# Sliding-window attention into an eight-expert MoE: late scatters ahead of later rooms' gathers, weight halves on one engine, scales built apart from row numbers

## The chip, the cores and the metric

One core of one Trainium2 chip runs the whole program in one launch. The metric is the device time of that launch in microseconds (us), lower is better. Engines are named as in the profile: PE multiplies matrices, ACT and DVE work on rows of 128 partitions, POOL does small elementwise work and issues every indexed DMA (gather, scatter), SP issues the plain DMAs.

## The reference

Attention of 8 batches, 8 heads, 576 tokens, 64 wide, with a window of 128 and a linear bias, and behind it a mixture of 8 experts:

```
scores = q @ k.T / 8 + bias          # only 0 <= i - j < 128
attn   = softmax(scores) @ v         # 8 x 8 x 576 x 64
x      = attn laid out as 8 x 576 x 512
logits = x @ w_gate ; local = sigmoid(x @ w_local)
for each batch, for s in 0..575:
    e = argmax(logits[s]) if s == 0 or local[s] < 0.5 else the expert of s - 1
    out[s] = softmax(logits[s])[e] * (relu(x[s] @ w1[e]) @ w2[e])
```

w1 is 8 x 512 x 1024, w2 is 8 x 1024 x 512, everything in fp32.

## The kernel before

**Attention, room by room.** A batch is called a room, numbered 0 to 7; a room has four slots of two heads. Each slot's atoms stand in a hand-written string (`ORDER`): scores `S`, row maximum on DVE, exponent on ACT, transposes and the product with v on PE. Generators that do other work are advanced at marks between the atoms: `.` is the routing of the room before (its `route`, its row copies and its entries), and from room 5 on `;` is `early`, `,` is `turns` and `:` is `gathers`. `queued` pins the order in which an engine's instructions were written, so an engine meets its instructions in that order, and an instruction that waits holds all that stand behind it on its engine.

**Routing.** For a room, `route` finds each token's expert, counts the tokens of each expert before it (`OH`, the one-hot of the choice, times a triangle on PE, plus the running counter row `ohs`), and writes each token's row number and its factor into `pay`. Five `enter` scatters of POOL (L725, `t<-pay,to`) put them into a table in HBM (`t4`, `t_76` in the order), sorted by expert. Entries not made at once wait in the list `late`. On POOL the room's outputs are also scaled (`product`, `T<-T,rn`, 128 x 576, four in a room) before SP stores them to `xd`, from which rows are gathered again.

**Experts.** The expert phase is a row of visits. Visits 0 to 3 take 384, 256, 256 and 256 tokens of four experts ("own", 36 columns of table) out of what rooms 0 to 4 hold. `early` does their tables once room 4 is entered: it raises the counters `ohs` of the four experts to the next full block (L877 to L884: for each, two tensor_scalar and one 1x1 add), loads four pieces of the table (`load_table`, L217, `xs<-t`, which waits for every entry made so far), spreads them over the partitions on PE and ACT (`copies`: `pk<-xs,rep`, `xt`), and `indices` makes of them row numbers to gather from (`xidx`) and, through `fw` on POOL and a reduce `sg` on DVE, scales and row numbers to scatter to. `gathers` then fetches visit 0's 12 pieces of rows into a spare buffer (`wraw<-xd,xidx`), and `turns` transposes its three tiles (`xtr`, L203, on DVE) and halves them into a rounded high part and a rest (`qx`, L207 on ACT and L209 on DVE).

**What a visit does.** `h<-qx,cut` and `y<-cut,hh` are its two products (L1100 to L1102, three matmuls for each block: high by high, high by low, low by high). ACT makes the high half of `h` (`hh`, L1205). A weight chunk is loaded by SP into one of six raw buffers (`wraw<-w`, L285), and `split_chunk` cuts it: ACT casts (L295), a subtract makes the rest (L297), on DVE for all halves but number `POOL_CUT = 19`, which POOL does.

**Order in the expert phase.** `Feed.tick` is called between blocks of matmuls. It advances room 7's routing (`side`), and every third tick or so sends one indexed DMA: a gather of a later visit's rows, or `other`, which is a scatter of finished rows (`out<-y`, L1085) or one of the `late` entries. It takes these by turns:

```
ahead_of = self.at < len(self.items) and self.items[self.at][0] <= upto or self.odd
first, second = (self.gather, self.other) if ahead_of else (self.other, self.gather)
```

**The tables of the last visits.** `rank_tables` runs at the end of `side`. It waits until `late` is empty and loads eight further pieces of the table (L217, the first two of 80 and 76 columns) for the experts ordered by their counts. These loads stand on SP in one queue with the weight loads, and wait for every entry.

Of the kernel before, what the change touches and what calls it, by code (L numbers as in the profile page):

```python
# [8 lines left out]
F32 = mybir.dt.float32  # L9
# [4 lines left out]
ALU = mybir.AluOpType  # L14
AX = mybir.AxisListType
PS = bass.MemoryType.PSUM
P = 128

NB = 8
S = 576  # L20
DM = 512
NE = 8
# [3 lines left out]
OWN = [(7, 384), (2, 256), (1, 256), (6, 256)]  # L26
# [5 lines left out]
BPE = 160  # L32
# [36 lines left out]
]  # L69
PLACE = [0, 8, 2, 1, 4, 3, 6, 5, 7]  # L70
DEPTH = 3
POOL_CUT = 19
HALVED = 8
FAR = 2.0 ** 40
Z_HOLD = -1.5 * 2.0 ** -23


@with_exitstack
def moe_attention(ctx, tc, qT, kT_d, vv, vt, wg, wl, w1, w2, out):
# [6 lines left out]
    tp = ctx.enter_context(tc.tile_pool(name="tok", bufs=2))  # L86
# [14 lines left out]
    own = cp.tile([P, NE], F32, name="own")  # L101
    caps = cp.tile([P, NE], F32, name="caps")
    rest = cp.tile([P, NE], F32, name="rest")
    starts = cp.tile([P, NE], F32, name="starts")
    msel = cp.tile([P, 4], F32, name="msel")
    roff = cp.tile([P, 1], F32, name="roff")
# [15 lines left out]
    ohs = st.tile([P, NE], F16, name="ohs")  # L122
# [65 lines left out]
    now = Now()  # L188
# [27 lines left out]
    def load_table(c0, n, block):  # L216
        ins = nc.sync.dma_start(xs[:, c0:c0 + n], t4v[:, block:block + n] if isinstance(block, int) else t4v[:, bass.ds(block, n)])  # L217
        for other in entered:
            tc.add_manual_dep(ins.ins, other.ins.name, mybir.DependencyInfo(mybir.DependencyClass.Sync, mybir.DependencyReason.DATA), reason="entries")
# [5 lines left out]
            tensor.matmul(pk[:, :m].rearrange("p c w -> p (c w)"), rep, xs[:, c:c + m].rearrange("p c w -> p (c w)"), start=True, stop=True)  # L225
            scalar.copy(xt[:, c:c + m], pk[:, :m])

    def indices(vector, c0, n, w0, wins, aid=None):

        aid = aid or vector  # L230
        vector.tensor_tensor(xidx[:, c0:c0 + n], xt[:, c0:c0 + n, 0], roff.broadcast_to([P, n]), ALU.add)
        yield
        m = len(wins)
        f = tp.tile([P, 48, 2, 4], F32, name="fw", bufs=1)[:, :m]
        lo = 0
        while lo < m:
            hi = lo + 1
            while hi < m and wins[hi] == wins[hi - 1] + 4:
                hi += 1
            for w in range(2):  # L240
                aid.tensor_tensor(f[:, lo:hi, w], xt[:, wins[lo]:wins[lo] + 4 * (hi - lo), 1 + w].rearrange("p (c q) -> p c q", q=4),
                                     msel.unsqueeze(1).broadcast_to([P, hi - lo, 4]), ALU.mult)
            lo = hi
            yield
        vector.tensor_reduce(sg[:, w0:w0 + m], f, AX.X, ALU.add)
        vector.tensor_copy(sidx[:, w0:w0 + m], sg[:, w0:w0 + m, 0])
        yield
# [42 lines left out]
                              reason="behind the values")  # L290
        return t

    def split_chunk(raw, c, scalar, vector, n):
        for f in range(2):
            scalar.copy(c[:, 0, f], raw[:, f])  # L295
            yield
            (pool if 2 * n + f == POOL_CUT else vector).tensor_tensor(c[:, 1, f], raw[:, f], c[:, 0, f], ALU.subtract)  # L297
            yield

    class Stream:  # L300
# [22 lines left out]
        def split(self, c, scalar, vector):  # L323
            raw = self.raw.pop(0)
            self.cut[self.n_cut] = c[:, 0], c[:, 1]
            self.n_cut += 1
            yield from split_chunk(raw, c, scalar, vector, self.n_cut - 1 if self is W else 0)

        def find(self, which):
            return min(i for i in self.cut if self.order[i][1] == which)  # L330
# [35 lines left out]
    with ExitStack() as actx:  # L366
# [271 lines left out]
        def lay_rows(b, g, copy):  # L638
            rows, rb = RN[b % 2][:, 0:72].rearrange("p (k i z) -> p k i z", k=4, z=2), RB[b % 2]
            for o in range(2):  # L640
                for z in range(2):
                    c = 64 * (g ^ o) + 32 * z
                    for a in range(2):
                        q = 64 * g + 32 * a
                        copy[a % len(copy)](rows[q:q + 32, :, o::2, z], rb[c:c + 32, :, o:9:2])

        def last_sums():
            b = NB - 1
            invert(b)
            yield  # L650
            both_engines = [dve.tensor_copy, act.copy]
            lay_by_head(b, both_engines)
            yield
            for g in range(2):
                lay_rows(b, g, both_engines)
                yield

        def tokens(b, xT):

# [38 lines left out]
        def scaled(b):  # L698

            if b < NB - 1:  # L700
                while b not in inverted:
                    yield
                for g in range(2):
                    lay_rows(b, g, [pool.tensor_copy])
                    yield
            stores.append(b)
            laid.append(b)
            if b == NB - 1:
                for _ in range(4 * now.calm):
                    yield  # L710
                for p in range(4):
                    product(b, p)
                    yield
                store(b)
# [22 lines left out]
        def in_turns(entries, products):  # L737
            entries, products = list(entries), list(products)
            while entries or products:
                if entries:  # L740
                    e = entries.pop(0)
                    if e == "row":
                        next(prep[":"], None)
                    else:
                        enter(*e)
                if products:
                    e = products.pop(0)
                    if e == "rest":
                        for _ in range(4):
                            pool.memset(spacer, 0.0)  # L750
                    else:
                        product(*e)

        def behind_choices(b):
            if b == NB - 2:
                in_turns(["row"] * 2 + late[:2], [(b, p) for p in range(4)])
                del late[:2]
            if b > NB - 3:
                return
            if b == NB - 3:  # L760
                in_turns(late + ["row"] * 4, [(b, p) for p in range(4)])
            else:
                in_turns(late, [(b, 0)] if b + 1 in EARLY else [(b, 0), (b, 1)])
            late.clear()

        def behind_counts(b):
            n = NT if b + 1 in EARLY else 3 if b < NB - 3 else 0
            late.extend((b, t) for t in range(n, NT))
            if n:
                in_turns([(b, t) for t in range(n)], [(b, p) for p in range(1 if n == NT else 2, 4)])  # L770
            elif b < NB - 1:
                k = 2 if b == NB - 3 else 4
                in_turns(["row"] * k, ["rest"] * (k - 1))

        def both(main, other):

# [93 lines left out]
        def early(group):  # L870
            while EARLY[group[0]] - 1 not in routed:
                yield
            while now.held:
                yield
            pn = ptk.tile([P, NE], F32, name="pk")
            pe.matmul(pn, onesb, ohs, start=True, stop=True)
            for i in group:  # L877
                e, k = OWN[i]
                d = tp.tile([P, 1], F32, name="ed")
                dve.tensor_scalar(d, pn[:, e:e + 1], -1.0, float(k + 32 * BPE * e), ALU.mult, ALU.add)  # L880
                dve.tensor_scalar(d, d, 0.0, None, ALU.max)
                dve.tensor_tensor(ohs[0:1, e:e + 1], ohs[0:1, e:e + 1], d[0:1], ALU.add)
                bumped.append(i)
                load_table(col_of[i], OWN_BLOCKS[i], BPE * e)  # L884
            while slot < LATE + 2 or now.held:
                yield
            copies(pe, act, col_of[group[0]], sum(OWN_BLOCKS[i] for i in group))
            yield
            for i in group:
                yield from indices(dve, col_of[i], OWN_BLOCKS[i], win_of[i], wins_of[i], pool)  # L890
                known.append(i)

        def gathers():

# [35 lines left out]
        side, prep = iter(()), {":": setup(), ";": iter(())}  # L930
        pairs = {}
        LATE = 4 * EARLY[0] + 4
        sums, SUMS = last_sums(), ("C1", "C2", "M1", "M2")

        def spread(order):
            for i, atom in enumerate(order.split()):
# [63 lines left out]
    def rank_tables():  # L1000
# [27 lines left out]
            nc.vector.tensor_scalar(efx[:, f:f + NE], er, 0.0, None, ALU.add)  # L1028
        yield
        while late:  # L1030
            yield
        for a, z, wait in ((0, 2, 8), (2, NE, 14)):
            for r in range(a, z):
# [284 lines left out]
    class Feed:  # L1318
# [52 lines left out]
        def tick(self, upto, turn=True):  # L1371

            self.clock += 1
            next(self.side, None)
            if route_done:
                now.act = nc.scalar
            if next(self.step, 0) == 0 and turn:
                self.turn(upto, 8 if upto == 1 else 10 if upto <= len(EARLY) else self.LAG)
            if upto > len(EARLY):
                self.drain()  # L1380
                self.gather(upto)
                if pending and self.clock % 3 == 0:
                    send()
            elif self.clock >= self.free:
                ahead_of = self.at < len(self.items) and self.items[self.at][0] <= upto or self.odd
                first, second = (self.gather, self.other) if ahead_of else (self.other, self.gather)
                if first(upto) or second(upto):
                    self.free, self.odd = self.clock + 2, not self.odd
# [92 lines left out]
```

## Time and profile before

| quantity | value |
|---|---|
| time, median of 3 runs | 693.24 us (693.11 to 694.29) |
| profiled execution: its time, its span | 693.75 us, 692.1 us |
| mean granted PE clock | 0.965 of full speed |
| PE busy | 650.5 us, 94% |
| DVE, ACT, POOL busy | 456.2, 417.3, 350.2 us |
| q1 (plain DMAs), q0 (indexed DMAs), share of 16 engines | 49.3%, 9.7% |

The time is the median of three runs; durations are read in the profiled execution, whose span is 692.1 us and whose own time is 1.65 us longer. Attention lasts until about 225 us, the end of attention and the first visit overlap until about 255 us, the rest is experts. PE is busy 94% of the span, so what can be saved without less matmul work is its idle time (41.6 us) and the time in which its clock was granted below full speed.

### The profile page before, as it was taken

To read this page: it belongs to the slowest core of one execution; us is meant where nothing else is said; L and a number is where in the kernel's file an instruction comes from. 1 tells how busy PE (TensorE), PEld (TensorE's weight loads), DVE (VectorE), ACT (ScalarE), POOL (GpSimd) and SP (SyncE) were. 2 spreads that over 40 slices of the span, in tenths; PEclk is the share of its full clock that TensorE was granted. 3 is DMA by queue.
4 is the path that set the end of the run, shared out by engine and by line. 5 is a ranking of instruction groups with operands and counts; after the bars stand their busy time and mean duration, and the time that the engine had idled before them with its cause. 6 is when DMAs were issued, how large, how long until landed. Compare 5 with 4: busy or idle time off the path is not lost. (4 is left out here: it accounts for less than half of the span.)

```text
span 692.1 us, 17132 instructions
## 1 busy us (share of the span) xinstructions
PE 650.5 (94%) x5928; PEld 536.7 (78%) x5928; DVE 456.2 (66%) x1445; ACT 417.3 (60%) x1239; POOL 350.2 (51%) x572
## 2 busy tenths in 40 slices
PE   8999999997959789996799999999999999999995
PEld 4777777775747668885689988888888888888884
DVE  6686876878637868883678856573645657476561
ACT  6889899896848674462556635363545455445541
POOL 6354655556363672676177776555463626141011
PEclk9999999998969879999799999999999999999998
DMA  7554784783766257542887856676675748455710
GB/s 232 187 187 149 237 270 150 230 265 108 250 197 201 83 162 256 160 147 82 310 260 245 254 184 180 200 248 201 205 240 170 261 155 289 143 171 166 273 35 32
DMA packets 50363, 134.42 MB, mean 194 GB/s; under 512 B 11015, under 2 KB 13703, under 8 KB 47970
## 3 DMA queue, kind: packets, MB, share of 16 engines
q1 hardware_dynamic: 40754, 113.43, 49.3%
q0 software_dynamic: 9088, 19.29, 9.7%
q8 instruction: 47, 0.77, 0.5%
q10 hardware_dynamic: 432, 0.59, 0.3%
q14 instruction: 42, 0.34, 0.2%
HBM read 113.67 MB, written 19.65 MB: 193 GB/s over the span
## 5 line engine op out<-in xcount | busy, mean ns | idle before, releaser
L197 POOL DMA_INDIRECT kr<-xd,xidx x137 | 155.3, 1133 | 58.5 <-issue 40.6
L297 DVE TENSOR_TENSOR cut<-wraw,cut 128x512 fp32r<-128x512 f32 x215 | 139.3, 685 | 51.2 <-ACT cut L295 50.2
L295 ACT CAST cut<-wraw 128x512 fp32r<-128x512 f32 x198 | 113.2, 617 | 46.7 <-PE y L1102 33.2
L1100 PE MATMUL h<-qx,cut 128*128 128x256 f32 (+8 forms) x440 | 139.5, 317 | 0.0
L1102 PE MATMUL h<-qx,cut 128*128 128x256 f32 (+8 forms) x440 | 138.2, 314 | 0.0
L1101 PE MATMUL h<-qx,cut 128*128 128x256 f32 (+8 forms) x440 | 138.2, 314 | 0.0
L172 ACT ACTIVATE cut<-scs,mn 128x192 f32<-128x192 f32 (+2 forms) x288 | 123.7, 434 | 22.4 <-DVE mn L172 21.6
L1100 PE MATMUL y<-cut,hh 128*128 128x512 f32 (+2 forms) x288 | 114.0, 396 | 9.8 <-ACT hh L1205 9.8
L1085 POOL DMA_INDIRECT out<-y,sidx x41 | 43.9, 1070 | 145.4 <-ACT y L1112 116.2
L1101 PE MATMUL y<-cut,hh 128*128 128x512 f32 (+2 forms) x288 | 113.8, 395 | 0.0
L1102 PE MATMUL y<-cut,hl 128*128 128x512 f32 (+2 forms) x288 | 113.2, 393 | 0.0
L1205 ACT ACTIVATE hh<-h 128x256 fp32r<-128x256 f32 (+7 forms) x104 | 46.0, 443 | 107.4 <-PE h L1102 107.0
L172 DVE CUSTOM_DVE_ANT_0 scs<-sc,bias 128x192 f32<-128x192 f32 (+2 forms) x288 | 84.2, 323 | 34.3 <-PE sc L172 19.7
L1206 DVE SCALAR_TENSOR_TENSOR hl<-h,hh 128x256 fp32r<-128x256 f32 (+8 forms) x112 | 55.6, 497 | 76.7 <-ACT hh L1205 71.9
L1100 PEld LDWEIGHTS h<-qx,cut 128*128 128x128 f32 x440 | 83.4, 190 | 12.9 <-issue 8.4
L172 PE MATMUL sc<-kr,qx 64*64 64x192 f32 (+2 forms) x1280 | 75.3, 315 | 12.2 <-DVE mn L172 11.7
L1101 PEld LDWEIGHTS h<-qx,cut 128*128 128x128 f32 x440 | 83.5, 190 | 3.7
L1102 PEld LDWEIGHTS h<-qx,cut 128*128 128x128 f32 x440 | 83.4, 190 | 0.1
L1100 PEld LDWEIGHTS y<-cut,hh 128*128 128x128 f32 (+2 forms) x288 | 53.8, 187 | 18.9 <-ACT hh L1205 10.2
L172 PEld LDWEIGHTS sc<-kr,qx 64*64 64x64 f32 x1280 | 45.8, 137 | 28.1 <-DVE mn L172 16.2
L172 PE MATMUL pt<-ident,cut 128*128 128x128 f32 x384 | 64.2, 292 | 1.0 <-ACT cut L172 0.7
L1102 PEld LDWEIGHTS y<-cut,hl 128*128 128x128 f32 (+2 forms) x288 | 53.7, 186 | 13.1 <-DVE hl L1206 0.5
(198 smaller groups left out, 936.1 us busy)
## 6 DMA issues: line engine op xcount, KB each, us to landing
wraw<-w SPq DMA_DIRECT2D x112, 512.0 KB
xT<-w SPq DMA_DIRECT2D x10, 1024.0 KB
kr<-kT SPq DMA_DIRECT2D x31, 288.0 KB
qx<-qT SPq DMA_DIRECT2D x30, 288.0 KB
xd<-T SPq DMA_DIRECT2D x7, 1152.0 KB
v<-v SPq DMA_DIRECT2D x22, 256.0 KB
v<-v SPq DMA_DIRECT2D x32, 128.0 KB
cut<-v SPq DMA_DIRECT2D x10, 256.0 KB
```

Of the source, the lines that this page charges most:

```text
L172: ins = getattr(self.engine, name)(*args, **kw)
L197: queued(nc.gpsimd.indirect_dma_start(out=r, out_offset=None, in_=src[0:n, :], in_offset=bass.IndirectOffsetOnAxis(ap=col, axis=0), bounds ...
L295: scalar.copy(c[:, 0, f], raw[:, f])
L297: (pool if 2 * n + f == POOL_CUT else vector).tensor_tensor(c[:, 1, f], raw[:, f], c[:, 0, f], ALU.subtract)
L1085: ins = nc.gpsimd.indirect_dma_start(out=out[:, :], out_offset=bass.IndirectOffsetOnAxis(ap=col[0:n], axis=0), in_=y[0:n], in_offset=None, ...
L1100: nc.tensor.matmul(o, ah, bh, start=start, stop=False)
L1101: nc.tensor.matmul(o, ah, bl, start=False, stop=False)
L1102: nc.tensor.matmul(o, al, bh, start=False, stop=stop)
L1205: now.act.activation(hh, hp, AF.Relu)
L1206: nc.vector.scalar_tensor_tensor(hl, hp, 0.0, hh, ALU.max, ALU.subtract)
```

## The change

Six edits. (1) The own tables' row numbers `xidx` are made in one instruction for all 36 columns, and the scales (`scales`: `fw` on POOL, `sg` on DVE) wait for a later slot (`LATE + 5`, the second slot of room 6), with twelve steps of the generator between POOL's part and DVE's. (2) The counters are raised by a subtract and a max over all eight experts on DVE and one add on POOL, in place of twelve DVE instructions. (3) No weight half is cut on POOL. (4) Row copies of the last room's sums move out of `last_sums` into the room's own side work. (5) The gathers of visit 0 come in fours: four with room 5's products as before, four behind room 5's counts, four with room 6's products; late entries that stood among them move behind room 6's counts. (6) In the expert phase a late entry goes ahead of gathers for later visits, and `rank_tables` waits ten ticks more once `late` is empty.

```diff
-POOL_CUT = 19
+WAIT = 10
...
-    def indices(vector, c0, n, w0, wins, aid=None):
-        aid = aid or vector
+    def indices(vector, c0, n, w0, wins):
         vector.tensor_tensor(xidx[:, c0:c0 + n], xt[:, c0:c0 + n, 0], roff.broadcast_to([P, n]), ALU.add)
         yield
+        yield from scales(vector, vector, w0, wins)
+    def scales(vector, aid, w0, wins):
         m = len(wins)
...
+        if aid is not vector:
+            for _ in range(12):
+                yield
         vector.tensor_reduce(sg[:, w0:w0 + m], f, AX.X, ALU.add)
...
-            (pool if 2 * n + f == POOL_CUT else vector).tensor_tensor(c[:, 1, f], raw[:, f], c[:, 0, f], ALU.subtract)
+            vector.tensor_tensor(c[:, 1, f], raw[:, f], c[:, 0, f], ALU.subtract)
...
             lay_by_head(b, both_engines)
             yield
-            for g in range(2):
-                lay_rows(b, g, both_engines)
-                yield
...
             if b == NB - 1:
-                for _ in range(4 * now.calm):
+                for g in range(2):
                     yield
+                    yield
+                    lay_rows(b, g, both_engines)
...
             if b == NB - 2:
-                in_turns(["row"] * 2 + late[:2], [(b, p) for p in range(4)])
-                del late[:2]
+                in_turns(["row"] * 4, [(b, p) for p in range(4)])
...
-                k = 2 if b == NB - 3 else 4
-                in_turns(["row"] * k, ["rest"] * (k - 1))
+                what = ["row"] * 4 if b == NB - 3 else late[:4]
+                in_turns(what, ["rest"] * 3)
+                if b == NB - 2:
+                    del late[:4]
...
+            d = tp.tile([P, NE], F32, name="ed", bufs=1)
+            dve.tensor_tensor(d, own, pn, ALU.subtract)
+            dve.tensor_scalar(d, d, 0.0, None, ALU.max)
+            pool.tensor_tensor(ohs[0:1], ohs[0:1], d[0:1], ALU.add)
             for i in group:
-                e, k = OWN[i]
-                d = tp.tile([P, 1], F32, name="ed")
-                dve.tensor_scalar(d, pn[:, e:e + 1], -1.0, float(k + 32 * BPE * e), ALU.mult, ALU.add)
-                dve.tensor_scalar(d, d, 0.0, None, ALU.max)
-                dve.tensor_tensor(ohs[0:1, e:e + 1], ohs[0:1, e:e + 1], d[0:1], ALU.add)
                 bumped.append(i)
-                load_table(col_of[i], OWN_BLOCKS[i], BPE * e)
+                load_table(col_of[i], OWN_BLOCKS[i], BPE * OWN[i][0])
...
-            for i in group:
-                yield from indices(dve, col_of[i], OWN_BLOCKS[i], win_of[i], wins_of[i], pool)
-                known.append(i)
+            c0, n = col_of[group[0]], sum(OWN_BLOCKS[i] for i in group)
+            dve.tensor_tensor(xidx[:, c0:c0 + n], xt[:, c0:c0 + n, 0], roff.broadcast_to([P, n]), ALU.add)
+            known.extend(group)
+            while slot < LATE + 5:
+                yield
+            yield from scales(dve, pool, win_of[group[0]], [w for i in group for w in wins_of[i]])
...
         while late:
             yield
+        for _ in range(WAIT):
+            yield
...
-                ahead_of = self.at < len(self.items) and self.items[self.at][0] <= upto or self.odd
+                ahead_of = self.at < len(self.items) and self.items[self.at][0] <= upto or self.odd and not late
```

Lines move down by 6 at L285 and L297 and by 11 at L1085 and L1100; the entries' L725 becomes L731.

**POOL in room 5.** The engine is POOL, the place is the end of room 5's products and what stands behind them; `wraw<-xd,xidx` are the gathers of visit 0's rows, `T` a product, `fw` the first half of the scales, `pay` to `ohs` room 5's row numbers and counts. Before:

```order
L197 DMA wraw<-xd,xidx 128x128
L172 TENSOR_TENSOR T_162<-T_162,rn_97 128x18x32
L172 TENSOR_TENSOR fw<-xt,msel 128x2x4 x4
L172 TENSOR_TENSOR pay<-gt,rse 128x5
L172 TENSOR_TENSOR ri<-ri,cblk 128x5
L172 TENSOR_TENSOR to<-ri,ki 128x5
```

and of the changed kernel:

```order
L197 DMA wraw<-xd,xidx 128x128
L172 TENSOR_TENSOR T_162<-T_162,rn_97 128x18x32
L172 TENSOR_TENSOR pay<-gt,rse 128x5
L172 TENSOR_TENSOR ri<-ri,cblk 128x5
L172 TENSOR_TENSOR to<-ri,ki 128x5
L172 TENSOR_TENSOR ohs<-ohs,cn 128x8
L197 DMA wraw<-xd,xidx 128x128
L172 MEMSET spacer 128x1 x4
L197 DMA wraw<-xd,xidx 128x128
L172 MEMSET spacer 128x1 x4
L197 DMA wraw<-xd,xidx 128x128
L172 MEMSET spacer 128x1 x4
```

The four small `fw` products no longer stand between the scaled rows and room 5's row numbers; they are part of one `fw` pair that comes behind the next four gathers, and two more gathers have moved up to that place.

**DVE in room 6.** The engine is DVE, the place is the one-hot `OH` of room 6's choices; `xtr` is the transposed tile of visit 0, `hr0` the scan of the sticky choice, `scs,mn` the scores with their row maximum. Before:

```order
854 L172 ISA mn_4883 128x1
855 L172 SCALAR_TENSOR_TENSOR hr0_105<-hold_4930,hr0_105,pk_4918 1x64
856 L203 STREAM_TRANSPOSE xtr_4965<-wraw_159 128x512
857 L209 TENSOR_TENSOR qx_4513<-xtr_4965,qx_4513 128x4x128
858 L172 TENSOR_TENSOR OH_4817<-pk_4968,k8_82 128x40
```

and of the changed kernel:

```order
837 L172 ISA mn_4871 128x1
838 L172 SCALAR_TENSOR_TENSOR hr0_105<-hold_4918,hr0_105,pk_4906 1x64
839 L203 STREAM_TRANSPOSE xtr_4953<-wraw_159 128x512
840 L172 TENSOR_TENSOR OH_4803<-pk_4956,k8_82 128x40
841 L172 ISA scs_4966,mn_4871<-sc_4925,bias_134 128x192
```

The transposition stands ahead of `OH` in both. Before it is visit 0's second tile, now the third and last; its `qx` now stands eleven rows behind `OH`.

**POOL and SP around room 7's entries.** The engine is POOL, the place is visit 1, the last stretch of entries; `kr<-xd,xidx` are gathers of later visits' rows. Before:

```order
L725 DMA t_76<-pay,to 40960x4
L197 DMA kr<-xd,xidx 128x128
L725 DMA t_76<-pay,to 40960x4
L197 DMA kr<-xd,xidx 128x128 x3
L1085 DMA out<-y,sidx 4608x512 x2
L725 DMA t_76<-pay,to 40960x4 x3
L1085 DMA out<-y,sidx 4608x512 x2
```

and of the changed kernel, from room 7's counts:

```order
L172 TENSOR_TENSOR ohs<-ohs,cn 128x8
L197 DMA kr<-xd,xidx 128x128
L731 DMA t_76<-pay,to 40960x4
L197 DMA kr<-xd,xidx 128x128 x7
L1096 DMA out<-y,sidx 4608x512
L731 DMA t_76<-pay,to 40960x4 x4
L1096 DMA out<-y,sidx 4608x512
```

Before, ten of the entries of rooms 5 to 7 stand behind room 7's counts, one by one between gathers; now five do, all of room 7. On SP, the two first tables of the last visits stand before:

```order
L285 DMA wraw<-w 128x1024 x2
L217 ISA
L217 DMA xs<-t_76 32x80
L217 ISA
L217 DMA xs<-t_76 32x76
L351 TENSOR_LOAD efx
```

and in the changed kernel:

```order
L217 ISA
L217 DMA xs<-t_76 32x80
L217 ISA
L217 DMA xs<-t_76 32x76
L1046 TENSOR_LOAD efx
L1046 ISA x2
L217 ISA
L217 DMA xs<-t_76 32x56
L1046 TENSOR_LOAD efx
L1046 ISA x2
L291 DMA wraw<-w 128x1024 x2
```

The same tables stand two weight loads earlier in SP's queue, with a third table behind them: the two loads that stood ahead now stand behind.

## Rows read from the trace of the kernel before

**Rows 1.** What PE waited for: us in total, times, longest.

```profile
PE sc L172 <- DVE mn L172: 11.7, 5, 6.9
...
PE y L1100 <- ACT hh L1205: 9.8, 1, 9.8
...
PE pk L172 <- DVE OH L172: 3.8, 7, 2.0
...
PE xa L172 <- ACT xT L172: 2.8, 2, 1.8
```

**Rows 2.** Stretches: length, busy of PE, PEld, DVE, ACT, POOL, PEclk, DMA.

```profile
170.51:176.44 5.93, 5.93 (x67) 4.41 (x67) 3.71 (x19) 5.30 (x21) 3.61 (x4) 0.57 0.51 201
...
232.94:250.62 17.68, 10.68 (x116) 6.98 (x112) 11.60 (x43) 9.73 (x33) 12.21 (x27) 0.71 0.24 86
...
250.62:254.18 3.56, 3.56 (x11) 3.33 (x11) 3.56 (x7) 3.56 (x7) 2.95 (x3) 0.50 0.81 208
...
332.35:335.94 3.59, 3.59 (x11) 2.85 (x12) 2.90 (x6) 2.07 (x5) 0.00 (x0) 0.50 0.92 325
...
335.94:680.00 344.06, 344.06 (x1872) 298.48 (x1872) 215.92 (x391) 173.86 (x365) 164.48 (x147) 1.00 0.62 204
```

**Rows 3.** Timeline of DVE: one transposition that each room has, rooms 4 to 7.

```profile
122.82 0.57 DVE L172 STREAM_TRANSPOSE T<-xT 128x384 f32<-128x384 f32 x1
...
149.65 0.57 DVE L172 STREAM_TRANSPOSE T<-xT 128x384 f32<-128x384 f32 x1
...
182.48 0.57 DVE L172 STREAM_TRANSPOSE T<-xT 128x384 f32<-128x384 f32 x1
...
220.78 0.57 DVE L172 STREAM_TRANSPOSE kr<-xT 128x384 f32<-128x384 f32 x1
```

**Rows 4.** Timeline of DVE and POOL, counters being raised: start, us, instruction.

```profile
165.86 1.64 DVE L172 TENSOR_TENSOR ohs<-ohs,ed 1x1 f16<-1x1 f16 x1
...
167.79 0.15 DVE L172 TENSOR_TENSOR ohs<-ohs,ed 1x1 f16<-1x1 f16 x1
...
166.28 1.20 POOL L172 TENSOR_TENSOR T<-T,rn 128x576 f32<-128x576 f32 x1
```

**Rows 5.** Timeline of SP and PE: the own tables.

```profile
176.88 1.73 SPq L217 DMA_DIRECT2D xs<-t  x4
...
183.96 0.51 PE L172 MATMUL pk<-xs,rep 32*128 32x144 f32 x2
```

**Rows 6.** Timeline of DVE: the reduce of the scales, with its wait.

```profile
200.07 0.17 DVE L172 TENSOR_REDUCE sg<-fw 128x4 f32<-128x16 f32 x1 [7.66 <-POOL fw L172]
```

**Rows 7.** Timeline of POOL and DVE: visit 0's second tile, room 6's choice.

```profile
229.87 1.04 POOL L197 DMA_INDIRECT wraw<-xd,xidx  x1 [0.16 <-issue]
...
232.46 0.71 DVE L203 STREAM_TRANSPOSE xtr<-wraw 128x512 f32<-128x512 f32 x1 [1.28 <-DMA wraw<-xd,xidx]
...
235.01 0.18 DVE L172 TENSOR_TENSOR OH<-pk,k 128x40 f16<-128x40 f32 x1
...
235.50 1.74 DVE L172 TENSOR_TENSOR rch<-rex,OH 128x40 f32<-128x40 f32 x1
```

**Rows 8.** Timeline of ACT: casts of weight halves, and its longest wait.

```profile
311.25 1.14 ACT L295 CAST cut<-wraw 128x512 fp32r<-128x512 f32 x2
...
330.88 1.14 ACT L295 CAST cut<-wraw 128x512 fp32r<-128x512 f32 x2 [13.50 <-DMA wraw<-w]
```

**Rows 9.** Timeline of SP: tables and the weight loads around them.

```profile
323.46 0.89 SPq L217 DMA_DIRECT2D xs<-t  x2
...
326.93 0.83 SPq L285 DMA_DIRECT2D wraw<-w  x2
```

**Rows 10.** Timeline of POOL: first and last entry behind room 7's counts.

```profile
285.36 1.03 POOL L725 DMA_INDIRECT t<-pay,to  x1 [0.49 <-issue]
...
321.24 0.91 POOL L725 DMA_INDIRECT t<-pay,to  x1 [0.30 <-issue]
```

**Rows 11.** Gathers by shape, POOL 285 to 325 us: busy, mean ns, idle before.

```profile
L197 POOL DMA_INDIRECT kr<-xd,xidx x13 | 14.8, 1138 | 4.0 <-issue 3.7 <-DMA kr<-xd,xidx 0.3
```

More of the change, by code (lines that the diff above doesn't have):

```diff
@@ L291, in load_chunk, with split_chunk @@
         return t
-    def split_chunk(raw, c, scalar, vector, n):
+    def split_chunk(raw, c, scalar, vector):
         for f in range(2):
@@ L326, in split @@
             self.n_cut += 1
-            yield from split_chunk(raw, c, scalar, vector, self.n_cut - 1 if self is W else 0)
+            yield from split_chunk(raw, c, scalar, vector)
         def find(self, which):
@@ L645, in lay_rows @@
                         copy[a % len(copy)](rows[q:q + 32, :, o::2, z], rb[c:c + 32, :, o:9:2])
+        both_engines = [dve.tensor_copy, act.copy]
         def last_sums():
@@ L650, in last_sums @@
             yield
-            both_engines = [dve.tensor_copy, act.copy]
             lay_by_head(b, both_engines)
             yield
-            for g in range(2):
-                lay_rows(b, g, both_engines)
-                yield
         def tokens(b, xT):
@@ L932, in moe_attention @@
         LATE = 4 * EARLY[0] + 4
-        sums, SUMS = last_sums(), ("C1", "C2", "M1", "M2")
+        sums, SUMS = last_sums(), ("C1", "C2")
         def spread(order):
```

## The prediction, made before the changed kernel ran

> **What bounds the kernel now.** I first looked for a stretch in which PE never waits, because what is saved ahead of such a stretch is carried to the end. The view by stretches has it: from 335.94 to 680.00 us PE is busy 344.06 of 344.06 us at clock 1.00 [rows 2]. The chain that ended last says nothing more than the last scatter. Next comes the list of PE's waits, which is short [rows 1]: 11.7 us for `mn`, of which one wait is 6.9; one wait of 9.8 us for `hh`; 3.8 us for `OH`, longest 2.0; 2.8 us for a transposed copy `xT`. All of it lies ahead of 336 us. A wait costs more than its length, because the granted clock falls behind it: 0.57 behind the first, 0.50 behind the last [rows 2]. The full price is read from a marker, a transposition that every room has at the same place: 122.82, 149.65, 182.48, 220.78 [rows 3]. An undisturbed room takes 26.83 us, the next ones 32.83 and 38.30, so two stalls cost 6.00 (stall A) and 11.47 us (B), clock included. Two further places are the end of attention, 17.68 us long with PE busy 10.68 at clock 0.71 (stretch C), and the wait of 9.82 us that ends at 332.35, with 3.59 us at half clock behind it (stall D) [rows 1, 2].
>
> **Stall A, counters raised at once.** From about 165.4 us DVE does the twelve counter instructions, with the third add at 167.79, and PE waits for the row maximum behind them. Two of the four 1x1 adds carry the length: 1.64 us against 0.15 for the same shape, with a product of 1.20 us on POOL beside it [rows 4]. The change leaves two small instructions on DVE, about 0.3 us, so the 6.00 us of the marker could come back. What is late next is the own tables: SP issues them at 176.88, and PE uses them (`pk<-xs,rep`) at 183.96 [rows 5]. If all 6.0 us came back PE would stand there at 177.96, while the tables, issued by the same last entry on POOL, are there at 176.88 + 1.73 for issuing four + about 2 for landing = 180.6. PE would wait 2.6 us, and some 0.1 more at a lower clock. **A gives 6.0 - 2.7 = 3.3 us.** Bounds: 6.0 if the entries, the add on POOL ahead of the tables and the tables also come earlier, 2.0 if the landing takes as long as a weight's 4 us.
>
> **Stall B, scales apart.** At 200.07 us DVE's reduce `sg` has waited 7.66 us for `fw` on POOL [rows 6], and behind it stand the scores that PE waits 6.9 us for [rows 1]. In POOL's order `fw` stands behind four gathers and four products, each pair about 2.4 us. The change puts all of `fw` behind room 5's counts and the next four gathers, and the reduce into room 6, twelve steps later. No DVE instruction that the scores need then waits for a late one of POOL here. What stays is that room 5's row numbers follow on POOL behind its products, and room 5's own small DVE work runs beside them. The nearest row is `rch` at 235.50, 1.74 us beside such a product [rows 7]; four products could each hold one, 4 x 1.2 = 4.8 us; I take 1.0, since most of DVE's work there reads the scores from PE's side. **B gives 11.47 - 1.0 = 10.5 us**, bounds 6.7 and 11.5.
>
> The Trainium skill ("SBUF — State Buffer", Who interferes with whom) says that a DVE instruction with two inputs in SBUF contends with a GpSimd instruction that reads SBUF, and that the second to issue is blocked for the whole of the other. The 1.64 us beside 0.15 agrees; taken strictly for room 5's four products this rule speaks against the change, and by it B would give 6.7 and the sum come out 3.8 us worse, an estimate.
>
> **Stretch C, first rows four by four.** Room 6's `OH` stands on DVE behind the transposition of a tile of visit 0. Before, that transposition had waited 1.28 us for its gathers, and `OH` ran at 235.01, behind a `qx` subtract too [rows 7]. The gather that released it was issued at 229.87, 2.6 us earlier [rows 7], the second behind room 6's choices. In the new order the tile there is the third, and its four gathers alternate with all of room 6's products. A gather (1.04 us) and a product (1.2 us [rows 4]) with their gaps make about 2.4 us, so in the clock of before they are issued at 227.5, 229.9, 232.3 and 234.7. The last lands at 234.7 + 2.6 = 237.3, the transposition takes 0.71, `OH` runs at about 238.1: PE's longest `OH` wait of 2.0 grows by 3.1 us. In exchange visit 0 is ready when attention ends. The 11 matmuls of 250.62 to 254.18 ran at 0.50 [rows 2] because the last tile was only then there; they can now fill gaps of C, worth at least 3.56 x 0.5 = 1.8 us and at most 3.6, and a wait of 1.4 us for that tile goes. The row copies that moved out of C shorten the 2.8 us of `xT` waits by perhaps half, 1.4. The sum is -3.1 + 1.8 + 1.4 + 1.4 = **1.5 us gained in C**; bounds 4 us lost (the `OH` wait and its clock, no copies ahead) to 4 us gained. Those copies reappear in visit 0, where PE is busy throughout and its `hh` and `hl` have room; they are counted at nothing, or 1.5 us lost.
>
> **Stall D, late scatters first.** The 13.50 us for which ACT waits before its cast at 330.88 [rows 8] is a wait for weights. In SP's queue the two tables stood ahead of them; these went at 323.46, and the two loads behind them at 326.93, landing 3.95 us later [rows 8, 9]. The tables waited for the last entry, issued at 321.24; room 7's first was issued at 285.36 [rows 10]. In between POOL alternates entries with gathers of visits not yet begun, at (14.8 + 4.0) / 13 = 1.45 us each [rows 11]. The new order has, behind room 7's counts, a gather, an entry, seven gathers, a scatter of results and four entries, fourteen DMAs. The last starts at 285.36 + 13 x 1.45 = 304.2, and the tables follow 2.2 us later as before, at 306.4 instead of 323.46.
>
> The tables also stand two loads earlier in SP's queue, with a third behind them, so the two loads that wait there are those that ACT cuts at 311.25 and next, not those of 317.38 (330.88 - 13.50). The first of them: three tables cost 3 x 0.45 and two scalar loads 2 x 0.65 (from 324.35 to 326.93 four such were issued), so it goes at 309.0 and lands at 312.9, 1.7 us behind the cast's place. PE ran dry only at 332.35 - 9.82 = 322.5, 5.1 us after ACT stopped, so it bears a landing until 316.3: it has 3.4 us of room. **D gives 9.82 + 3.59 x 0.5 = 11.6 us**, bounds 11.6 and 5.
>
> The rest is small: the half that POOL cut comes to DVE, 0.7 us in a visit where PE is the bound; nothing. Gathers of visits 1 and 2 give way to ten entries of 1.45 us; PE's list of waits names no gathered rows of a later visit [rows 1], and the eight that visit 2 needs first stand ahead of the last entries, done by about 304, where the last entry goes, while visit 1 lasts beyond the casts at 311; hidden.
>
> **Rivals.** *R1, the table wait still starves weights.* If POOL starts late (a blocked gather, or 3 entries more), the last entry comes after 307.6 and a wait returns, one for one, with its clock: 5 to 11 us of D are lost and the time is 672 to 678. For it speaks that SP now stops two loads earlier; against it the 3.4 us of room. *R2, room 6 waits for the third tile.* C loses 3 to 5 us in place of gaining 1.5: 671. For it speaks that the second tile's transposition already waited 1.28 us for its gathers; against it the work of visit 0 that may fill the wait. *R3, products hold DVE in room 5, or the own tables hold PE in A,* the far bounds of A and B: 670. By the rule named above R3 is the likelier form of B. *R4, the other side: the table loads block the weights for longer than before.* Everything gained ahead of visit 1 (15 us) would have to be lost there. SP would have to hold at the tables until 323.46 + 15 - 4 (two loads earlier) = about 334, some 28 us beyond 306.4, which at 1.45 us are 19 more indexed DMAs ahead of the last entry than the order shows. A single cause for it would be entries that wait on gathered rows being free; the order shows none. *R5, the change does not do what it says,* the waits standing as before: within 0.5 us of before. The order of POOL and DVE speaks against it.
>
> **How the numbers follow.** The sum is 3.3 + 10.5 + 1.5 + 11.6 = 26.9 us against the profiled execution's 693.75: 666.9; that run is 0.5 us over the median, so **666.5 us** is predicted. Chances: the forecast 0.58, between 661 and 672 by the bounds of A to C; R1 0.17; R2 0.12; R3 0.08; R4 0.03; R5 0.02. The low end takes the best bounds, 6.0 + 11.5 + 4 + 11.6 = 33.1, that is 660; the high end takes R1's middle with R2's loss, 678. Between 659 and 679 lies all but R4, R5 and a tail of R1. A measurement of this kernel tells 0.2% from no change; faster by more is 0.94, within it 0.02, slower 0.04.
>
> **What would show it.** Right: in the list of PE's waits no `mn` wait over 3 us and no `hh` wait over 3; room periods of 27 to 31 us; the tables 80 and 76 issued near 306 - 15 = 291 us on SP and no wait of ACT for `wraw` near 13 us; `sg` without a wait for `fw`. Wrong: a wait for `pk<-xs` over 4 us (A), an `OH` wait over 6 us (C), or SP standing at `xs<-t` with ACT waiting for `wraw` again (D).

## The result, and the profile after

| | before | changed |
|---|---|---|
| median, us | 693.17 (4 runs, 691.04 to 694.29) | 674.70 (4 runs, 673.59 to 676.81) |
| profiled execution: time, span, us | 693.75, 692.1 | 676.81, 675.1 |
| mean granted PE clock | 0.965 | 0.983 |
| PE busy, us | 650.5 | 644.7 |

The ratio of the times is 0.9741 (95% interval 0.9707 to 0.9774), 18.5 us less at the median. 666.5 was forecast, so 8.2 us of the forecast gain did not come. The profiled execution of the changed kernel is the slowest of its four, 2.1 us over the median, and sums below are made against its span.

What PE waits for in the changed kernel (us in total, times, longest), to be held against [rows 1]:

```profile
PE pk L172 <- DVE OH L172: 7.2, 7, 5.4
...
PE pk L172 <- DMA xs<-t: 3.3, 1, 3.3
...
PE sc L172 <- DVE mn L172: 3.2, 5, 1.1
...
PE y L1111 <- ACT hh L1216: 1.9, 1, 1.9
...
PE pk L172 <- DVE hr L172: 1.6, 1, 1.6
```

The two large waits, 6.9 us for `mn` and 9.8 us for `hh`, are gone. What is read next is what stands in their place: 5.4 us for room 6's `OH`, 3.3 us for the own tables `xs`, 1.9 us for `hh`, 1.6 us for `hr`. The marker of [rows 3], in the changed kernel:

```profile
149.82 0.57 DVE L172 STREAM_TRANSPOSE T<-xT 128x384 f32<-128x384 f32 x1
...
179.07 0.58 DVE L172 STREAM_TRANSPOSE T<-xT 128x384 f32<-128x384 f32 x1 [1.37 <-ACT part L172]
...
213.14 0.57 DVE L172 STREAM_TRANSPOSE kr<-xT 128x384 f32<-128x384 f32 x1
```

and the first `y` matmul of visit 0, of the kernel before and then of the changed one:

```profile
256.97 0.50 PE L1100 MATMUL y<-cut,hh 128*128 128x512 f32 x1
```

```profile
245.71 0.50 PE L1111 MATMUL y<-cut,hh 128*128 128x512 f32 x1
```

Four intervals come out of these, and they add up to the 17.0 us between the two spans.

| interval | before | changed | gained | forecast |
|---|---|---|---|---|
| two rooms (stalls A and B), marker to marker | 71.13 | 63.32 | 7.8 | 13.8 |
| last marker to visit 0's first y (C) | 36.19 | 32.57 | 3.6 | 1.5 |
| first y to the end of the span (D) | 435.13 | 429.39 | 5.7 | 11.6 |
| start to first marker | 149.65 | 149.82 | -0.2 | 0 |

So 6.0 us are missing in A and B, 5.9 in D, and C gave 2.1 more than was forecast. The experiments are about these three.

### The profile page after: what moved, and what is told of

Read it like the earlier page. It is cut to its first block, busy times and chain, and to the rows that moved or that the text cites. A ratio compares the mean times of both kernels' runs of the same rounds, so it can differ in the third digit from the quotient of the medians.

```text
span 675.1 us, 17115 instructions
## 1 busy us (share of the span) xinstructions
PE 644.7 (95%) x5928; PEld 532.5 (79%) x5928; DVE 452.8 (67%) x1427; ACT 417.3 (62%) x1239; POOL 349.3 (52%) x574
## 5 line engine op out<-in xcount | busy, mean ns | idle before, releaser
L172 DVE CUSTOM_DVE_ANT_0 scs<-sc,bias 128x192 f32<-128x192 f32 (+2 forms) x288 | 83.8, 323 | 32.6 <-PE sc L172 19.7
L1111 PEld LDWEIGHTS y<-cut,hh 128*128 128x128 f32 (+2 forms) x288 | 53.7, 186 | 10.5 <-ACT hh L1216 2.4
```

Source lines behind the costliest of these rows:

```text
L172: ins = getattr(self.engine, name)(*args, **kw)
L1111: nc.tensor.matmul(o, ah, bh, start=start, stop=False)
```

## The experiments

The kernels did not all run on the same chip, and chips differ: the kernel before took 693.8 us where the changed kernel and three variants of it ran and 693.3 where the last kernel did, but 750.0 where its single parts ran and 736.3 where three later ones did. Each ratio is against the kernel before on the same chip, and intervals of the trace are compared with a control from the same chip.

**One part alone, on the kernel before (where it took 749.98 us).** Counters at once (part 2), scales apart (part 1), gathers in fours (part 5), late entries first (part 6), each with the lines of the change's diff and no other; of part 6:

```diff
-                ahead_of = self.at < len(self.items) and self.items[self.at][0] <= upto or self.odd
+                ahead_of = self.at < len(self.items) and self.items[self.at][0] <= upto or self.odd and not late
```

Counters. 

> The kernel before with the counters raised at once and nothing else. By the prediction's term A the time falls by 3.3 us, to about 690. By the reading of the changed trace (PE then waits for the own tables, and the clock falls behind that wait, so that nothing is left) it falls by less than 1.5 us: the wait before the scores at 170 us goes, and a wait of 2 to 4 us for xs appears about 10 us later.

Measured 748.75, ratio 0.9998 (0.9964 to 1.0032): not to be told from no change, and the 3.3 us of term A lie outside the interval (2.7 us gained to 2.4 lost). The 3.4 us wait at stall A is gone and PE waits 1.99 us for `xs` instead. Marker to marker the two rooms take 28.74 + 40.25 = 68.99 us, where the kernel with late entries first, which leaves both places as they were, takes 33.21 + 38.52 = 71.73: 2.7 us less, of which nothing shows in the median. (The kernel with the scales apart, which also leaves the first place as it was, takes 32.40 us there, so some 0.8 us of such a difference are spread.)

Scales. 

> The kernel before with the scales apart from the row numbers and nothing else. By the prediction's term B the time falls by 10.5 us, to about 682.7. By the rival in which products on POOL hold DVE's two-input instructions one each, it falls by only 6.7, to about 686.5.

Measured 739.74, ratio 0.9884 (0.9786 to 0.9981). Its markers:

```profile
150.81 0.57 DVE L172 STREAM_TRANSPOSE T<-xT 128x384 f32<-128x384 f32 x1
...
183.21 0.57 DVE L172 STREAM_TRANSPOSE T<-xT 128x384 f32<-128x384 f32 x1
...
212.94 0.57 DVE L172 STREAM_TRANSPOSE kr<-xT 128x384 f32<-128x384 f32 x1
```

The second interval is 29.73 us against 38.52 in the same control, so the scales alone are worth 8.8 us there, between the two figures that were laid down. The interval of the time, 1.4 to 16 us gained, holds both figures; it is the markers that tell.

Fours. 

> The kernel before with visit 0's gathers in fours and nothing else. By the prediction's term C the time falls by 1.5 us, to about 691.7; by the interval between the same two marks of the changed trace (room 6's transposition to the first y matmul) it falls by 3.6, to about 689.5; if the row copies or the scales were what helped there, it rises by 1 to 3, since room 6's OH then waits about 5 us.

Measured 749.88, ratio 1.0005 (0.9966 to 1.0045): nothing to be told. `OH` waits 5.4 us as forecast; by itself the edit buys nothing that a measurement on this chip shows, and of the figures laid down only the gain of 3.6 us lies outside the interval (2.5 us gained to 3.4 lost).

Late entries. 

> The kernel before with late entries ahead of later gathers and ten ticks more before the tables, and nothing else. By the prediction's term D the time falls by 11.6 us, to 681.6. If the two weight loads that now stand behind the tables still starve ACT, as in the changed trace, it falls by 5.5 to 8 us, to 685 to 688, and PE waits 1.5 to 4 us for hh once.

Measured 744.33, ratio 0.9919 (0.9877 to 0.9962), some 6 us, which is the size of the second forecast; the 11.6 us of term D lie outside the interval (2.9 to 9.2 us). On this chip it can't be read as one wait: PE's waits for weights come again and again through the expert phase (us in total, times, longest),

```profile
PE y L1102 <- ACT hh L1207: 17.0, 7, 5.2
...
PE y L1102 <- issue: 14.2, 4, 9.3
```

and where the kernels with the counters and the scales changed wait 12.6 and 14.0 us once, near 315 and 310 us, this one waits 9.3, so that part of the stall is still there.

**The changed kernel again, and three variants of it (before: 693.82 us).**

> The changed kernel unaltered, for a second profile. If the 4.9 us that the last own entry took to land in the first profile was that execution's alone, the tables are issued about 2 us behind the last entry, PE waits less than 1 us for them, and room 5's interval (from the marker transposition of one room to the next) shortens by 3 us or more. If the wait belongs to the kernel, it is again 2 to 4 us with half clock behind it.

Measured 674.11 (ratio 0.9714, 0.9698 to 0.9730), `xs` wait 3.17 us: the wait belongs to the kernel. The clock behind it is 0.69 for 5.48 us here, where the first profile has 0.50. The intervals are 62.20, 32.46 and 431.6 us, where the first profile has 63.32, 32.57 and 429.39: one profile's interval can be off by 1 to 2 us. This run is the control of the next three.

```diff
             while slot < LATE + 2 or now.held:
                 yield
+            for _ in range(4):
+                yield
             copies(pe, act, col_of[group[0]], sum(OWN_BLOCKS[i] for i in group))
```

> The changed kernel, the spreading of the own tables on PE four generator steps (about 4.5 us) later. If the tables are what stall A's gain went into, the wait for xs and the low clock behind it go: 4 to 6 us faster than the changed kernel. If visit 0's gathers are late next for it, the OH wait of room 6 grows instead and less than 2 us are left.

Measured 672.43 (0.9677, 0.9652 to 0.9702), 1.7 us less than the control; the two intervals overlap at their edges, but each of its four runs is below each of the control's. The `xs` wait is gone, but PE now waits 1.3 us at the same instruction for `lg`, which DVE had ahead:

```profile
183.78 0.48 PE L172 MATMUL pk<-xs,rep 32*128 32x144 f32 x2 [1.34 <-DVE lg L172]
```

The size is that of the second forecast, under 2 us, but not its reason: room 6's `OH` waits 5.4 us as in the control. The two rooms take 59.39 us against the control's 62.20, 2.8 us less, of which 1.7 show in the median.

```diff
-                for _ in range(6):
+                for _ in range(9 if t == 2 else 6):
                     yield
                 for _ in r.turn(t):
```

> The changed kernel, the third tile's transposition three generator steps later, behind room 6's OH and its last scores on DVE. If OH is held by that transposition's wait for its gathers, PE's OH wait falls from 5.4 us to about 0.3, and the time by 3 to 8 us (wait and clock). If visit 0 needs the tile at once, the wait moves to its first h and less than 2 us are gained.

Measured 671.55 (0.9686, 0.9666 to 0.9705), 2.6 us less than the control, with each run below each of the control's, and between the two forecasts. The `OH` wait falls to 0.3 us, and one of 3.1 us for a copy, `pts`, has taken the larger part of its place:

```profile
231.98 0.64 PE L172 MATMUL xa<-pts,v 128*64 128x64 f32 x11 [3.13 <-ACT pts L172]
...
228.36 1.31 DVE L172 TENSOR_TENSOR ki<-ri,c 128x5 int32<-128x5 int32 x1
...
230.31 0.46 ACT L172 ACTIVATE cut<-scs,mn 128x192 f32<-128x192 f32 x1 [1.28 <-DVE mn L172]
```

That copy stands on ACT behind an exponent that waits for DVE's row maximum, and DVE has just spent 1.31 us in `ki`, which takes 0.16 us in this room of the changed kernel; so what held DVE in room 5 has come up here as well. A copy of the same kind on DVE, behind the third tile's transposition, ends at the same moment (231.87), so the two can't be told apart as the cause. The wait for `hr` in visit 0 fell to 0.2 us with it: the last of visit 1's gathers is issued at 254.90 there, and its transposition at 257.36 waits for nothing.

The last of the four puts the loop of twelve counter instructions back into the changed kernel.

> The changed kernel with the counters raised by the twelve DVE instructions of before. By the prediction's term A it is 3.3 us slower than the changed kernel. If the own tables bound that place whichever way the counters are raised, it is within 1.5 us of it: 3.4 us of wait for the row maximum come back, the wait for xs goes.

Measured 675.86 (0.9747, 0.9730 to 0.9763), 1.7 us more than the control, with intervals that touch: between the two forecasts, and hardly told from nothing. Marker to marker its two rooms take 62.05 us, the control's 62.20. PE waits 3.39 us for the row maximum and not at all for the tables:

```profile
170.10 0.54 PE L172 MATMUL sc<-kr,qx 64*64 64x192 f32 x4 [3.39 <-DVE mn L172]
...
173.29 0.92 POOL L731 DMA_INDIRECT t<-pay,to  x1 [0.30 <-issue]
...
176.44 2.46 SPq L217 DMA_DIRECT2D xs<-t  x4
```

**What is left of D, and the late tables (before: 736.26 us).** The first holds the tables of the last visits behind two more weight loads by an order of issue on SP, the second does the counters' add on DVE, the third joins the three moves (copies four steps later, third tile three steps later, tables behind 23 loads).

```diff
+        if behind:
+            tc.add_manual_dep(ins.ins, behind.ins.name, mybir.DependencyInfo(mybir.DependencyClass.NoSync, mybir.DependencyReason.DATA), reason="behind weights")
...
-            pool.tensor_tensor(ohs[0:1], ohs[0:1], d[0:1], ALU.add)
+            dve.tensor_tensor(ohs[0:1], ohs[0:1], d[0:1], ALU.add)
```

> The changed kernel with the first three tables of the last visits held behind two more weight loads in SP's queue, the place they had before. If the rest of stall D is those two loads standing behind the tables, PE's wait for hh (1.9 us) and the half clock behind it go: 2 to 4 us faster than the changed kernel. If weights are late for another reason, the wait stays and the time is within 1 us of it.

Measured 721.99 (0.9820, 0.9777 to 0.9863). Inconclusive: on this chip PE waits 10.2 us for `hh` near 312 us although the tables stand behind these loads, and the changed kernel itself has no run there.

> The changed kernel with the counters' add on DVE in place of POOL, so that it no longer stands on POOL behind the last own entry. If POOL's elementwise work right behind the last entry delays that entry's landing (4.4 to 4.9 us here, 2.2 before), the landing goes back towards 2.2 and the wait for xs shrinks by about 2 us; the add itself may hold DVE for one product, 1.2 us. If the landing has another cause, it stays above 4 us and the time is within 1 us of the changed kernel.

Measured 724.91 (0.9864, 0.9827 to 0.9902), a time that has no changed kernel beside it on this chip. The tables went 4.2 us behind the end of the last entry, with the add off POOL:

```profile
174.73 0.92 POOL L731 DMA_INDIRECT t<-pay,to  x1 [0.30 <-issue]
...
179.83 1.27 SPq L217 DMA_DIRECT2D xs<-t  x3
```

The add on POOL is not what delays the landing.

> The changed kernel with three moves together: the own tables spread four steps later, the third tile turned three steps later, the tables of the last visits behind two more weight loads. If the three waits are separate, the gains add: about 2 + 2.7 + 2 to 4, a time of 666 to 668. If one takes the place of another, it is no better than the best of them, about 671.

Measured 715.67 (0.9723, 0.9662 to 0.9783). Its two rooms take 59.40 us, 3.6 less than the 63.02 of the kernel with only the tables moved; the weights' waits hide the rest. It was therefore run once more.

> The kernel with the three moves once more, since the chip of its first run was slower for every kernel. Where the kernel before takes 693 us, separate waits give 666 to 668 us and no wait of PE for hh near 300 us; one wait in the place of another gives 670 to 672.

Measured 665.02 (before: 693.32; ratio 0.9598, 0.9573 to 0.9623), 28.3 us less than before, the fastest version of all and better than either forecast. Its largest waits of PE:

```profile
PE xa L172 <- ACT pts L172: 3.1, 1, 3.1
...
PE sc L172 <- DVE mn L172: 3.1, 5, 1.1
...
PE pk L172 <- DVE OH L172: 2.0, 7, 0.3
...
PE pk L172 <- DVE lg L172: 1.2, 1, 1.2
```

No wait for `hh`, `xs` or `hr` is above 0.3 us. The tables went at 289.49, with two loads ahead of them:

```profile
280.64 2.20 SPq L295 DMA_DIRECT2D wraw<-w  x2
...
289.49 1.39 SPq L217 DMA_DIRECT2D xs<-t  x3
```

The three waits did not take one another's place: 28.3 us against the 19.7 of the changed kernel (693.82 to 674.11) are 8.6 us more, and the 1.7 and 2.6 us of the two moves that were measured alone leave about 4 for the third and for whatever the three give only together. Its markers on either side of the two rooms and its first `y`:

```profile
149.72 0.57 DVE L172 STREAM_TRANSPOSE T<-xT 128x384 f32<-128x384 f32 x1
...
208.74 0.57 DVE L172 STREAM_TRANSPOSE kr<-xT 128x384 f32<-128x384 f32 x1
...
239.05 0.50 PE L1120 MATMUL y<-cut,hh 128*128 128x512 f32 x1
```

So its two rooms take 59.02 us, the next interval 30.31 and the rest, to the end of its span at 663.2, 424.15. Held against the kernel before these are 12.1, 5.9 and 11.0 us gained, where 13.8, 1.5 and 11.6 had been forecast for the changed kernel: with the new waits out of the way, A with B and D come close to the sizes that were foreseen.

## Why the prediction came out as it did

**Place and direction were right; A, B and D were too large, C too small.** The stalls named are the ones that went, in each interval. Of the signs laid down, these came: the longest `mn` wait is 1.1 us, the `hh` wait 1.9, ACT's longest wait for weights 3.3, and `sg` waits for nothing. Two did not: the second room takes 34.07 us, where 27 to 31 were named, and the tables go at 297.52, not near 291. (The terms as written add up to 666.4, not 666.5, which changes nothing.)

**A (3.3 us forecast): the step that failed is the size of what is late next.** The tables were named as the next bound, with a cost of 2.7 us. They came later, and cost more:

```profile
165.77 1.91 DVE L172 TENSOR_SCALAR ed<-ed 128x8 f32<-128x8 f32 x1
...
166.44 1.19 POOL L172 TENSOR_TENSOR T<-T,rn 128x576 f32<-128x576 f32 x1
...
173.86 0.92 POOL L731 DMA_INDIRECT t<-pay,to  x1 [0.30 <-issue]
...
179.40 1.73 SPq L217 DMA_DIRECT2D xs<-t  x4
...
182.42 0.81 PE L172 MATMUL pk<-xs,rep 32*128 32x144 f32 x2 [3.27 <-DMA xs<-t]
```

```profile
182.42:188.00 5.58, 5.58 (x37) 3.74 (x38) 2.83 (x13) 3.24 (x14) 1.52 (x8) 0.50 0.89 284
```

The last entry starts at 173.86, as before, but the tables go 4.62 us after its end, not 2.25, so PE waits 3.27 us; and behind that wait lie 5.58 us at clock 0.50, 2.8 us lost, where the sum had put 0.1. Together these are 6.1 us (4.9 in the second profile). The landing itself, which no row had shown and which was put at about 2 us, took 1.3 (179.40 + 1.73 to 182.42). PE also came to the place only 5.0 us earlier by the marker, at 179.15, not 6.0: of the two small instructions, put at 0.3 us together, the second took 1.91 and ended with the product on POOL, where the like one of before, on one column, took 0.15. So A is worth about nothing, or 1 us lost in this profile, which with the 8.8 us of the scales is the 7.8 that the two rooms gained. That A is worth nothing there is shown by putting the twelve instructions back: the two rooms take the same time; in the whole time the 1.7 us between the medians are all that could be A's, and they are hardly told from nothing. It also fits what the counters gave alone. The clock behind a wait was read for the stalls of before [rows 2, 3] and then left out for the wait that was forecast: it belongs to the price on either side of the sum.

**B (10.5): 8.8 us alone.** The residual of 1.0 was too small; 2.7 us stayed. In room 5 DVE's small operations run beside POOL's products:

```profile
197.08 0.94 DVE L172 TENSOR_TENSOR rch<-rex,OH 128x40 f32<-128x40 f32 x1
...
199.06 1.31 DVE L172 TENSOR_TENSOR ki<-ri,c 128x5 int32<-128x5 int32 x1
...
200.41 0.17 DVE L172 TENSOR_TENSOR ri<-ri,c 128x5 int32<-128x5 int32 x1
...
199.18 1.16 POOL L172 TENSOR_TENSOR T<-T,rn 128x576 f32<-128x576 f32 x1
...
201.03 0.54 PE L172 MATMUL sc<-kr,qx 64*64 64x192 f32 x4 [1.10 <-DVE mn L172]
```

`ki` takes 1.31 us, the like operation behind it 0.17; `rch` takes 0.94 against 0.19 in the next room, and PE waits 1.10 us behind them. Two of the four products hold one operation each, where the bound had been four and the sum about one. Where the rest of the 2.7 us lies was not traced. The Trainium skill ("SBUF — State Buffer", Who interferes with whom) has this as DVE's second SBUF input being locked out while GpSimd reads; `ki`, which ends with the product of 199.18, agrees in length, though by the recorded starts it was the first of the two by 0.12 us. One held operation for each product, the 6.7 us of the prediction, was too much here.

**C (1.5): 3.6 us.** The loss was right: `OH` behind the third tile, a wait of 5.43 us where 5.1 were forecast.

```profile
231.40 0.71 DVE L203 STREAM_TRANSPOSE xtr<-wraw 128x512 f32<-128x512 f32 x1 [6.62 <-DMA wraw<-xd,xidx]
...
232.04 0.16 DVE L172 TENSOR_TENSOR OH<-pk,k 128x40 f16<-128x40 f32 x1
...
232.25 0.19 PE L172 MATMUL pk<-OH,utri 128*128 128x40 f16 x1 [5.43 <-DVE OH L172]
```

The gain was too small. Visit 0's h matmuls start at 238.68, ahead of the last products with v, and stand where PE had waited for copies of `xT`: of those 2.8 us [rows 1] nothing is left in the list, and the matmuls that ran at half clock from 250.62 [rows 2] run at full clock (columns as in [rows 2]):

```profile
238.68 0.45 PE L1111 MATMUL h<-qx,xT 128*128 128x384 f32 x1
```

```profile
238.00:246.00 8.00, 7.91 (x81) 6.03 (x80) 7.13 (x18) 7.58 (x20) 6.34 (x14) 1.00 0.54 146
```

How much of it is due to the moved row copies was not tried alone.

**D (11.6): 5.7 us, by two waits that had been counted as hidden.** The first is new. The gathers of visit 1 now go behind the entries of rooms 5 and 6. Before, the last of eight was issued 1.2 us after visit 0's first y; now it is 15.5:

```profile
261.20 1.00 POOL L197 DMA_INDIRECT kr<-xd,xidx  x1 [0.31 <-issue]
...
261.32 0.71 DVE L203 STREAM_TRANSPOSE xtr<-kr 128x512 f32<-128x512 f32 x1 [1.47 <-DMA kr<-xd,xidx]
...
265.05 0.19 PE L172 MATMUL pk<-identb,rcb 128*1 128x64 f16 x1 [1.65 <-DVE hr L172]
```

DVE holds the transposition of visit 1's tile until it lands, and behind it stands room 7's `hr`, for which PE waits 1.65 us (2.4 in the second profile). The prediction had said of these gathers that PE's list of waits did not name them; it could not, since nothing then delayed them. The second is what the first rival named, weights that come late behind the tables, but not by its cause, a late POOL:

```profile
294.68 1.39 POOL L731 DMA_INDIRECT t<-pay,to  x1 [0.30 <-issue]
...
297.52 2.36 SPq L217 DMA_DIRECT2D xs<-t  x3
...
300.58 0.36 SPq L291 DMA_DIRECT2D wraw<-w  x1
...
305.29 1.14 ACT L301 CAST cut<-wraw 128x512 fp32r<-128x512 f32 x2 [3.29 <-DMA wraw<-w]
...
306.76 0.50 PE L1111 MATMUL y<-cut,hh 128*128 128x512 f32 x1 [1.94 <-ACT hh L1216]
```

```profile
306.76:310.90 4.14, 4.01 (x13) 3.19 (x14) 2.37 (x5) 1.25 (x3) 3.23 (x4) 0.60 1.00 328
```

The last entry starts 18.5 us behind the first DMA that follows room 7's counts, as computed (18.85). But the tables went 2.84 us behind its start in place of 2.2, the load 3.06 us behind the tables in place of 2.65, and it landed 4.7 us later in place of 3.95, so ACT's cast came 3.29 us late where 1.7 had been computed. The step that failed here is the 3.4 us of room that were to bear it. PE ran dry at 304.82, 2.8 us after ACT had stopped at 302.00, where the sum took over the 5.1 us of the old place; and the sum left out the 1.47 us from the cast to the matmul behind it (305.29 to 306.76, and 330.88 to 332.35 before). 3.29 - 2.82 + 1.47 are the 1.94 us that PE waited, with 4.0 us of work at a mean clock of 0.60 behind. The two waits and that clock are 1.65 + 1.94 + 1.6 = 5.2 of the 5.9 us that are missing. In the version with the tables behind those two loads the wait for `hh` does not occur; that move was not measured alone where the kernel before takes 693 us, so its 4 us are a remainder and not a measurement.

**The rivals.** What R1 (weights starve, 0.17) and R3 (tables and products hold, 0.08) feared each came in part, R2's cost (room 6's `OH`) came in full but was outweighed. None decided by itself. The measured 674.70 lies outside the 661 to 672 that stood for the forecast itself; the range of 659 to 679 held because it reached to the rivals. That C gave 2.1 us more than its term, and so made up for part of what A, B and D fell short, was luck.

## What to carry to other kernels

When a stall goes, compute the arrival of the thing behind it and price its wait with the low clock that follows, exactly as the old one was priced; here the new wait was worth as much as the old. Work that goes ahead in a queue delays what it passes: ask for each passed transfer which in-order engine holds for it, not whether it was waited for before. And test parts together with what follows them: the counters alone gave nothing that could be measured, the moved copies, tile and tables gave 8.6 us more on top of the change.

## What was not expected of the hardware

The last own entry took 4.1 to 4.6 us from the end of its issue to the tables' start in all nine profiles of the seven kernels that raise the counters at once, and 2.2 to 2.3 us in all five that don't. It isn't POOL's add. The traces name a candidate: between the first piece of the rows' store `xd<-T` and the last piece of that entry, each of the nine profiles has a load of instructions, 16 KB in one packet of 0.88 us, and none of the five has one. In the second profile of the changed kernel, for the stretch 175.89 to 176.84, at whose end the entry's last pieces move:

```profile
q8 instruction: 1, 0.02, 5.8%
```

In the nine the entry's last piece moves 2.8 to 3.8 us behind the end of its issue, in the five 1.6. No run moved that load by itself, so the cause stays open.

And the same kernel before took 693, 736 and 750 us on different chips. On the slower two ACT stood in the expert phase for a releaser that the profile calls only "remote", in the kernel with scales apart

```profile
ACT hh L1214 <- remote: 56.8, 9, 17.2
```

which no profile on the faster chips shows (us in total, times, longest). What it waited for there can't be told from the trace.
